# Moving four steps in the last units of an attention and soft-mixture kernel

## The chip, the core and the metric

The kernel runs on one core of one Trainium2 chip. The metric is device time in microseconds (us); lower is better. Times quoted from inside an execution are microseconds from the start of the profiled span.

## What is computed

The reference is an attention with one extra term in the softmax denominator, followed by a mixture of eight small expert networks on 32 slots:

```python
q, k, v : (8, 12, 448, 64) float32          # batch, heads, sequence, head size
scores = scale * q @ k^T ; m = max(scores, -1) ; e = exp(scores - m)
attn = e / (sum(e, -1) + exp(-m) + 1e-9) ; x = (attn @ v) as (3584, 768)
logits = x @ phi                             # phi (768, 32)
d = softmax of logits over the 3584 rows ; slot_input = d^T @ x   # 8 experts x 4 slots
slot_out[e] = relu(slot_input[e] @ w1[e]) @ w2[e]   # w1 (8,768,1024), w2 (8,1024,768)
out = softmax of logits over the 32 slots @ slot_out
```

## The kernel before

**Units and steps.** The attention is cut into 24 units `u`. A unit is two batches by two heads (six head pairs for each of four batch pairs). A unit takes seven steps `t`, one for each block of 64 positions, so step `n = 7*u + t` runs up to 168. The kernel's order is written out by hand: `at(n, where, f)` puts work into a plan, and one loop over `n` issues it in the order "small", scores of step `n`, "value", second scores of step `n - 10`, "value", "end", "load". Each engine then runs its own instructions strictly in that order and waits on semaphores.

**The stages of a unit.**
- `load_qk`, `load_v`: the loads of a unit (`load`, L124). Queries and keys are issued by POOL, values by SP, in two transfers each. All values but those of unit 23 go through the one buffer `vr`, so a load of values waits until the cast of the unit before has read it.
- `stage_T` (L226, L229): transposes of queries and keys on PE, copied out by DVE.
- `stage_S` (L238, L242, L246): scores on PE, their row maximum on DVE.
- `stage_MT` (L250 to L269): the maxima transposed on PE, copied, and spread by POOL into `md` (L258, L264).
- `stage_ST` (L276, L281, L285): the scores once more, transposed, minus the maximum, on PE; the exponential on ACT.
- `stage_V` (L290): POOL casts the unit's values to bf16 beside a column of ones. It waits for both transfers of `load_v`.
- `stage_AV` (L312): exponentials times values on PE, into one accumulator `av`.
- `stage_AVout` (L323, L326): `av` copied to `xu`, of which there is one buffer, by ACT, or by DVE for unit 22.
- `stage_den` (L332, POOL), `stage_N` (L338 reciprocal on DVE, L340 product): the normalised output `x`. L340 is "unit N's product" below. It is the last reader of `xu`, so the copy-out of the next unit waits for it. `stage_last` does the same for unit 23 on DVE.
- `stage_X` (L392, L393): `x` transposed on PE and copied, for the logits (L424).

After every six units `mixture` brings the slot softmax up to date. After the last one follow the slot inputs, the experts' hidden layer (L658), the second layer (`outer`, L762) and the combination (L819, L823), whose tiles SP writes out.

**The expert weights.** They come in 32 pieces of 768 KB (bf16; they are cast on the way by the transfer itself), all issued by POOL in `load_w` (L166). Numbers 0 to 23 are resident: they have a place of their own in `wres`, and one or two are issued per unit from unit 2 on, the last one in unit 22. Numbers 24 to 31 are called late pieces 0 to 7 here: `room(i)` gives them 3072 columns of `block`, the tile that holds the attention's working buffers, so each waits until those buffers have been read for the last time. Late piece 0 lies over `vr` and unit 21's queries and keys, piece 1 over `qr` and `kr` (there unit 23's values land, too), piece 2 over unit 22's queries and keys and `md`, piece 3 over unit 22's cast values and `xu`. Pieces 4 to 7 are needed in the last part of `outer`.

Of the kernel before, what the change touches and what calls it, by code (L numbers as in the profile page):

```python
# [23 lines left out]
def kernel(  # L24
# [10 lines left out]
    nc = tc.nc  # L35
# [7 lines left out]
    TB = S // P  # L43
# [4 lines left out]
    U = BP * HP  # L48
# [40 lines left out]
    def buf(name, i):  # L89
        o, n, bufs = parts[name]  # L90
        return block[:, ds(o + (i % bufs) * n, n)]

    def xbuf(u):
        return block[:, ds(xbuf_at((u + 4) % (HP + 1)), N2)]
# [16 lines left out]
    def room(i):  # L111

        return wres[:, i, :] if i < WRES else block[:, ds(rooms[i - WRES], HW)]
# [14 lines left out]
    def load_qk(u):  # L128

        for src, name in ((q, "qr"), (k, "kr")):  # L130
            RAW[u, name] = load(u, buf(name, 0).rearrange("p (h n) -> p h n", h=2), src, nc.gpsimd)
# [13 lines left out]
    def load_v(u):  # L145
        t_ = block[:, ds(parts["vr" if u < U - 1 else "qr"][0], 2 * N2)].bitcast(F32).rearrange("p (h n) -> p h n", h=2)
        RAW[u, "vr"] = load(u, t_, v, nc.sync if u else nc.gpsimd)
# [7 lines left out]
    def load_w(i):  # L155


        kind, e, half = weights[i]
        if kind == 1:
            J, n = KC // 2, F  # L160
            src = moe_w1[e].rearrange("(p j) f -> p j f", p=128)[:, ds(half * J, J), :]
        else:
            J, n = FK // 2, DD
            src = moe_w2[e, ds(half * 128 * J, 128 * J)].rearrange("(p j) f -> p j f", p=128)
        t_ = room(i).rearrange("p (j n) -> p j n", n=n)
        gdma(out=t_, in_=src)  # L166
        for j in range(J):
            W[kind, e, half * J + j] = t_[:, j, :]
# [51 lines left out]
    def stage_T(u, name):  # L220

        ps = slot([128, 2, S], BF16)
        r = RAW.pop((u, name))
        for t in range(TB):
            for h in range(2):
                nc.tensor.transpose(ps[ds(h * D, D), :, ds(t * P, P)],  # L226
                                    r[:, h, ds(t * D, D)], ident)
        t_ = buf(f"qk{u % 3}", 0)[:, ts(int(name == "kr"), N2)].rearrange("p (b n) -> p b n", b=2)
        nc.vector.tensor_copy(t_, ps)  # L229
        (QT if name == "qr" else KT)[u] = t_  # L230
# [17 lines left out]
    def stage_MT(u):  # L248
        ps = slot([128, 128], BF16)
        nc.tensor.transpose(ps, M[u % 2], ident)  # L250
        mt = small.tile([128, 128], BF16, tag="mt", name="mt", bufs=1)
        (nc.scalar.copy if u < U - 1 else nc.vector.tensor_copy)(mt, ps)  # L252
        em = small.tile([128, 2, TB], F32, tag="em", name="em", bufs=3)
        nc.scalar.activation(em, M[u % 2].rearrange("p (h r) -> p h r", h=2)[:, :, ds(0, TB)],
                             AF.Exp, scale=-scale)
        EM[u] = em
        md = buf(f"md{u % 2}", 0).rearrange("p (b n) -> p b n", b=2)
        nc.gpsimd.tensor_tensor(  # L258
            md[:, :, ds(0, C3 * 128)].rearrange("p b (c n) -> p b c n", c=C3),
            mt.unsqueeze(1).unsqueeze(1).broadcast_to([128, 2, C3, 128]),  # L260
            nmask[:, ds(0, 2 * C3)].rearrange("p (b c) -> p b c", b=2).unsqueeze(3)
                 .broadcast_to([128, 2, C3, 128]),
            op=ALU.mult)
        nc.gpsimd.tensor_tensor(  # L264
            md[:, :, ds(C3 * 128, P)], mt.rearrange("p (b n) -> p b n", b=2),
            nmask[:, ds(2 * C3, 1)].unsqueeze(2).broadcast_to([128, 2, P]), op=ALU.mult)
        MD[u] = md
        if u < U - 1:
            nc.gpsimd.tensor_scalar(em, em, 1e-9, None, op0=ALU.add)  # L269
# [18 lines left out]
    def stage_V(u):  # L288
        t_ = buf(f"v6{5 + u % 2}", 0).rearrange("p (h t e) -> p h t e", h=2, e=66)
        nc.gpsimd.tensor_copy(t_[:, :, :, ds(0, D)],  # L290
                              RAW.pop((u, "vr")).rearrange("p h (t d) -> p h t d", t=TB))
        if u < 2:
            nc.gpsimd.memset(t_[:, :, :, ds(D, 1)], 1.0)
        V65[u] = t_

    def stage_AV(u, ts_, part):

        for t in ts_:  # L300
            if t == 0 and part == 0:
                AV[u] = pav.tile([128, 2, 512], F32, tag="av", name="av")
            av, et = AV[u], ET[u, t]
            for h in range(2):
                for c in (range(C3) if part == 0 else (C3,)):
                    for b in range(2):
                        bs = ds(b * P, P)
                        if c < C3:
                            o, w = av[:, b, ds((h * C3 + c) * 65, 65)], 128
                        else:  # L310
                            o, w = av[bs, h, ds(2 * C3 * 65, 65)], P
                        nc.tensor.matmul(o, et[bs, h, ds(c * 128, w)],  # L312
                                         V65[u][bs, h, t, ds(0, 65)],
                                         start=(t == 0 and h == 0 and c == 0),
                                         stop=(t == TB - 1), skip_group_check=True)
            if part == 1:
                ET.pop((u, t))

    def stage_AVout(u):
        av = AV.pop(u)  # L320
        xu = buf("xu", 0).bitcast(F32).rearrange("p (h s e) -> p h s e", h=2, e=65)
        copy = nc.scalar.copy if u < U - 2 else nc.vector.tensor_copy
        copy(  # L323
            xu[:, :, ds(0, 2 * C3), :].rearrange("p h (b c) e -> p b h (c e)", b=2),
            av[:, :, ds(0, 2 * C3 * 65)].rearrange("p b (h e) -> p b h e", h=2))
        copy(xu[:, :, TB - 1, :], av[:, :, ds(2 * C3 * 65, 65)])  # L326
        XU[u] = xu

    def stage_den(u):
        xu = XU[u]  # L330
        den = small.tile([128, 2, TB], F32, tag="den", name="den")
        nc.gpsimd.tensor_tensor(den, xu[:, :, :, D], EM.pop(u), op=ALU.add)  # L332
        DEN[u] = den

    def stage_N(u):
        xv = XU.pop(u)
        rec = small.tile([128, 2, TB], F32, tag="rec", name="rec", bufs=1)
        nc.vector.reciprocal(rec, DEN.pop(u))  # L338
        x = xbuf(u).rearrange("p (s n) -> p s n", s=TB)
        (nc.gpsimd if u < U - 2 else nc.vector).tensor_tensor(  # L340
            x.rearrange("p s (h d) -> p h s d", h=2), xv[:, :, :, ds(0, D)],
            rec.unsqueeze(3).broadcast_to([128, 2, TB, D]), op=ALU.mult)
        X[u] = x
# [349 lines left out]
    def at(n, where, f):  # L693
        plan.setdefault((n, where), []).append(f)

    for u in range(U):
        n = u * TB
        if u + 1 < U:
            at(n + 5, "value", lambda u=u: [stage_T(u + 1, name) for name in ("qr", "kr")])
        if u + 2 < U:  # L700
            at(n + 5, "load", lambda u=u: load_qk(u + 2))
        at(n + 7, "value" if u < U - 1 else "small", lambda u=u: stage_MT(u))
        at(n + (9 if u < U - 1 else 5), "load", lambda u=u: stage_V(u))
        if u + 1 < U:
            at(n + (9 if u < U - 2 else 5), "load", lambda u=u: load_v(u + 1))
        for m in sorted(set(AV0)):
            at(n + m, "value", lambda u=u, m=m: [
                stage_AV(u, [t for t in range(TB) if AV0[t] == m], part) for part in range(2)])
        if u < U - 1:
            at(n + 19, "small", lambda u=u: stage_AVout(u))  # L710
            at(n + 20, "value", lambda u=u: stage_den(u))
            at(n + (23 if u < U - 3 else 22 if u < U - 2 else 21), "small", lambda u=u: stage_N(u))
        else:
            at(n + 11, "load", lambda u=u: last_sinks(u))
            at(n + 19, "small", lambda u=u: stage_last(u))
        if u < U - 2:
            at(n + 26, "value", lambda u=u: stage_X(u))
        else:
            at(n + (24 if u == U - 2 else 26), "end", lambda u=u: stage_X(u))
# [1 line left out]
        mixture(bp, (bp * HP + HP - 1) * TB + 27, at)  # L721

    for i, u in enumerate(sorted((*range(2, U - 1), 9, 13, 16))):
        at(u * TB + 5, "load", lambda i=i: load_w(i))
    at(4, "load", late_constants)
    stage_T(0, "qr")
    stage_T(0, "kr")

    end = TB * U
    for n, i in ((end - 5, 0), (end - 1, 1), (end + 3, 2), (end + 7, 3), (end + 12, 4),  # L730
                 (end + 12, 5)):
        at(n, "load", lambda i=i: load_w(WRES + i))
    at(end + 2, "load", first_spread)
# [121 lines left out]
```

## Time and profile before

| | us |
|---|---|
| median of 3 runs | 327.3 (325.09 to 332.09) |
| the profiled execution, its own time | 326.59 |
| its span, first to last instruction | 324.7 |
| PE busy in the span | 280.2 (86%) |
| DVE busy | 254.6 (78%) |
| ACT busy | 213.7 (66%) |
| POOL busy | 207.3 (64%) |

The work with units runs to about 270 us of the span, the slots and experts from there to about 295 us, and the rest writes the output. All four steps that the change touches lie between 245 and 270 us. The busy shares are means over the whole span, so they say little about that stretch; the views of the prediction are taken from it.

### The profile page before, as it was taken

The page shows a single profiled execution, that of the slowest core. Times are in us where ns is not written, and L with a number is a line of the kernel's source. Part 1 is how long each engine was busy: PE and PEld are TensorE (multiplying, and loading weights), DVE is VectorE, ACT ScalarE, POOL GpSimd, SP SyncE. Part 2 cuts the span into 40 slices and gives each one's busy share as a digit, 9 for nine tenths or more (in the row PEclk, how much of TensorE's full clock was granted, in tenths as well). Part 3 has the DMA queues.
Part 4 walks back from the last instruction along what each step waited for, and adds up shares of the span by engine and source line. Part 5 has one row for each costly group of instructions (what it writes and reads, how often), then busy time and mean ns, then how long its engine had stood idle before and what let it go on. Part 6 is the DMA issues. An engine that isn't in the chain of part 4 may idle for free.

```text
span 324.7 us, 13074 instructions
## 1 busy us (share of the span) xinstructions
PE 280.2 (86%) x5793; PEld 159.0 (49%) x5794; DVE 254.6 (78%) x354; ACT 213.7 (66%) x341; POOL 207.3 (64%) x308
## 2 busy tenths in 40 slices
PE   1669999999999988999989999998999897987910
PEld 1325555555655555556655555565555454452300
DVE  2988999898998988889989898888998844416820
ACT  3026877877778776877777778776877884216610
POOL 6356677797877786888867877968684663310000
PEclk9999999999999999999999999999999997999555
DMA  7355789998889799998997899987988599976998
GB/s 137 67 82 92 125 169 184 164 191 159 168 169 172 126 188 206 198 176 168 192 230 123 160 206 231 186 164 148 183 132 170 113 198 209 212 152 246 399 399 315
DMA packets 30311, 59.31 MB, mean 183 GB/s; under 512 B 4048, under 2 KB 22736, under 8 KB 30256
## 3 DMA queue, kind: packets, MB, share of 16 engines
q0 software_dynamic: 19056, 36.46, 65.3%
q1 hardware_dynamic: 11200, 22.02, 21.2%
q8 instruction: 45, 0.74, 0.9%
q14 instruction: 10, 0.08, 0.1%
HBM read 83.46 MB, written 11.01 MB: 291 GB/s over the span
## 4 chain that ended last, share of the span: by engine, by line
PE 57%; DVE 15%; POOL 7%; issue 6%; DMA 5%; ACT 5%; SPq 0%; ACTq 0%; POOLq 0%; DVEq 0%
PE av L312 14%; PE ps L276 10%; PE ps L238 10%; DVE m L246 8%; PE ps L281 8%; PE ps L226 6%; ACT block L285 5%; DMA block<-in_moe_w_dram 4%; PE ps L819 4%; DVE block L229 2%; PE ps L242 2%; POOL block L258 2%; POOL block L340 2%; DMA wres<-in_q_dram 1%; POOL block L124 1%
## 5 line engine op out<-in xcount | busy, mean ns | idle before, releaser
L246 DVE TENSOR_REDUCE m<-ps 128x2 bf16<-128x896 f32 x168 | 180.6, 1090 | 23.5 <-PE ps L238 19.4
L285 ACT ACTIVATE block<-ps 128x896 bf16<-128x896 f32 x168 | 153.8, 917 | 53.0 <-PE ps L281 49.1
L312 PE MATMUL av<-block 64*128 64x65 bf16 (+1 forms) x2688 | 83.7, 193 | 2.2 <-issue 1.9
L312 PEld LDWEIGHTS <-block 64*128 64x128 bf16 (+1 forms) x2688 | 70.8, 97 | 28.2 <-issue 10.1
L276 PE MATMUL ps<-block,ones 64*64 64x448 bf16 x672 | 69.1, 368 | 5.1 <-POOL block L264 2.3
L281 PE MATMUL ps<-block 64*64 64x448 bf16 x672 | 66.1, 353 | 0.2 <-issue 0.2
L238 PE MATMUL ps<-block 64*128 64x448 bf16 x288 | 54.4, 371 | 3.0 <-DVE m L246 1.3
L124 POOL DMA_DIRECT2D block<-in_q_dram x46 | 29.5, 644 | 30.9 <-PE ps L226 30.8
L238 PEld LDWEIGHTS <-block 64*128 64x128 bf16 x288 | 19.8, 94 | 52.3 <-issue 51.3
L258 POOL TENSOR_TENSOR block<-mt,nmask 128x768 bf16<-128x768 bf16 x24 | 35.7, 1487 | 9.2 <-ACT mt L252 7.8
L340 POOL TENSOR_TENSOR block<-block,rec 128x896 bf16<-128x896 f32 x22 | 37.1, 1688 | 1.4
L276 PEld LDWEIGHTS <-ones 64*64 64x64 bf16 x672 | 24.6, 105 | 10.2 <-issue 5.3
L229 DVE COPY block<-ps 128x896 bf16<-128x896 bf16 x48 | 27.8, 616 | 0.8 <-PE ps L226 0.5
L124 POOL DMA_DIRECT2D block<-in_k_dram x46 | 27.9, 627 | 0.0
L226 PE MATMUL ps<-ident,block 128*64 128x128 bf16 x644 | 25.5, 228 | 2.7 <-ACT block L285 0.5
L226 PEld LDWEIGHTS <-block 128*64 128x64 bf16 x644 | 23.0, 114 | 5.8 <-issue 2.7
L290 POOL CAST block<-block 128x896 bf16<-128x896 f32 x24 | 22.3, 931 | 3.5 <-PE ps L392 2.0
L281 PEld LDWEIGHTS <-block 64*64 64x64 bf16 x672 | 24.0, 107 | 0.6 <-issue 0.6
L323 ACT COPY block<-av 128x780 f32<-128x780 f32 x22 | 17.7, 804 | 0.0
L252 ACT COPY mt<-ps 128x128 bf16<-128x128 bf16 x23 | 6.1, 265 | 17.4 <-PE ps L250 16.8
L392 PE MATMUL ps<-ident,block 128*128 128x128 bf16 x168 | 13.4, 219 | 3.5 <-POOL block L340 1.1
L166 POOL DMA_DIRECT2D wres<-in_moe_w_dram x24 | 14.6, 617 | 1.8 <-issue 1.8
(144 smaller groups left out, 249.0 us busy)
## 6 DMA issues: line engine op xcount, KB each, us to landing
wres<-in_moe_w_dram POOLq DMA_DIRECT2D x24, 768.0 KB, 9.2
out_dram<-wres SPq DMA_DIRECT2D x28, 384.0 KB, 4.2
block<-in_v_dram SPq DMA_DIRECT2D x46, 224.0 KB, 4.6
block<-in_moe_w_dram POOLq DMA_DIRECT2D x8, 768.0 KB, 9.4
block<-in_q_dram POOLq DMA_DIRECT2D x46, 112.0 KB, 4.1
block<-in_k_dram POOLq DMA_DIRECT2D x46, 112.0 KB, 4.8
wres<-in_q_dram SPq DMA_DIRECT2D x2, 224.0 KB, 4.1
block<-in_v_dram POOLq DMA_DIRECT2D x2, 224.0 KB, 3.6
```

The costliest lines, as they stand in the source:

```text
L124: eng.dma_start(out=t_[ds(b * P, P), :, :], in_=src[bp * 2 + b, ds(hp * 2, 2)].rearrange("h (p t) d -> p h (t d)", t=TB))
L226: nc.tensor.transpose(ps[ds(h * D, D), :, ds(t * P, P)], r[:, h, ds(t * D, D)], ident)
L229: nc.vector.tensor_copy(t_, ps)
L238: nc.tensor.matmul(ps[:, h, ds(0, S)], QT[u][hs, b, ds(c * 128, 128)], KT[u][hs, b, :], start=True, stop=True)
L246: nc.vector.tensor_reduce(m[:, :, s], ps[:, :, ds(0, S)], axis=AX.X, op=ALU.max)
L258: nc.gpsimd.tensor_tensor(md[:, :, ds(0, C3 * 128)].rearrange("p b (c n) -> p b c n", c=C3), mt.unsqueeze(1).unsqueeze(1).broadcast_to([12 ...
L276: nc.tensor.matmul(ps[ds(b * P, P), h, ds(0, S)], ones[hs, :], MD[u][hs, b, :], start=True, stop=False)
L281: nc.tensor.matmul(ps[ds(b * P, P), h, ds(0, S)], KT[u][hs, b, ds(t * P, P)], QT[u][hs, b, :], start=False, stop=True)
L285: nc.scalar.activation(et, ps[:, :, ds(0, S)], AF.Exp, scale=scale)
L290: nc.gpsimd.tensor_copy(t_[:, :, :, ds(0, D)], RAW.pop((u, "vr")).rearrange("p h (t d) -> p h t d", t=TB))
L312: nc.tensor.matmul(o, et[bs, h, ds(c * 128, w)], V65[u][bs, h, t, ds(0, 65)], start=(t == 0 and h == 0 and c == 0), stop=(t == TB - 1), sk ...
L340: (nc.gpsimd if u < U - 2 else nc.vector).tensor_tensor(x.rearrange("p s (h d) -> p h s d", h=2), xv[:, :, :, ds(0, D)], rec.unsqueeze(3). ...
```

## The change

Four steps move, all in units 21 to 23:
- the last resident piece is issued at step 160 in place of 159;
- the cast of unit 22's values (the last but one) is planned at step 162 in place of 163;
- the late pieces 1 and 2 are planned at steps 166 and 170 in place of 167 and 171;
- unit 21's product (L340) goes from POOL to DVE; units 22 and 23 already had theirs there.

```diff
@@ stage_N
-        (nc.gpsimd if u < U - 2 else nc.vector).tensor_tensor(
+        (nc.gpsimd if u < U - 3 else nc.vector).tensor_tensor(
             x.rearrange("p s (h d) -> p h s d", h=2), xv[:, :, :, ds(0, D)],
             rec.unsqueeze(3).broadcast_to([128, 2, TB, D]), op=ALU.mult)
@@ the plan
-        at(n + (9 if u < U - 1 else 5), "load", lambda u=u: stage_V(u))
+        at(n + (9 if u < U - 2 else 8 if u < U - 1 else 5), "load", lambda u=u: stage_V(u))
@@
     for i, u in enumerate(sorted((*range(2, U - 1), 9, 13, 16))):
-        at(u * TB + 5, "load", lambda i=i: load_w(i))
+        at(u * TB + (5 if u < U - 2 else 6), "load", lambda i=i: load_w(i))
@@
-    for n, i in ((end - 5, 0), (end - 1, 1), (end + 3, 2), (end + 7, 3), (end + 12, 4),
+    for n, i in ((end - 5, 0), (end - 2, 1), (end + 2, 2), (end + 7, 3), (end + 12, 4),
                  (end + 12, 5)):
```

PE, ACT and SP run the same instructions in the same order. DVE has one instruction more (unit 21's product). POOL's order in the stretch, as its queue has it (den, md and product are L332, L258 with L264, and L340):

```
before: product 19, cast 21, RESIDENT, den 20, md 22, product 20, CAST 22, late 0, cast 23,
        den 21, LATE 1, md 23, PRODUCT 21, memset and copies, LATE 2, copies, den 22, late 3
after:  product 19, cast 21, den 20, RESIDENT, md 22, CAST 22, product 20, late 0, cast 23,
        LATE 1, den 21, md 23, LATE 2, memset and copies, copies, den 22, late 3
```

## The prediction

> **What bounds the kernel now.** I read the chain that ended last, backwards from the end, then each engine's timeline from 245 to 270 us, then the DMA view in windows of 1 us. The chain's last wait for a transfer, with start, duration and what:
>
> ```profile
> 277.94 0.52 POOL block L166
> 278.46 12.94 DMA block<-in_moe_w_dram
> 291.40 0.04 issue
> 291.44 1.47 PE ps L762 x29
> ```
>
> PE waits for late piece 7, which lands at 291.40. The page gives that wait as 0.84 us, so PE was ready at 290.59, and no gain from the pieces alone can pass 0.85 us. Every us by which PE itself comes later than 290.59 counts from 291.44 on; the output behind it is the same work. So two clocks matter: when PE gets there, and when piece 7 lands. The eight pieces stand back to back on the DMA engines (share 1.0 from 260 to 289). Issues and landings (median time to landing by window): piece 0 257.44 and 264.2, piece 1 259.29 and 268.3, piece 2 264.08 and 272.8, piece 3 268.52 and 276.5, then one every 3.7 us. A piece with nothing ahead lands 6.8 us after its issue (piece 0), otherwise about 4 us after the one ahead.
>
> POOL's timeline (start, duration, instruction, idle before it) shows what makes piece 0 late:
>
> ```profile
> 245.30 0.62 POOL L166 DMA_DIRECT2D wres<-in_moe_w_dram  x1
> 246.14 0.22 POOL L332 TENSOR_TENSOR den<-block,em 128x14 f32<-128x14 f32 x1 [0.22 <-ACT block L326]
> 252.56 1.69 POOL L340 TENSOR_TENSOR block<-block,rec 128x896 bf16<-128x896 f32 x1
> 256.21 0.93 POOL L290 CAST block<-block 128x896 bf16<-128x896 f32 x1 [1.97 <-PE ps L392]
> 257.44 0.61 POOL L166 DMA_DIRECT2D block<-in_moe_w_dram  x1 [0.30 <-PE ps L242]
> ```
>
> The cast at 256.21 is unit 22's. Its 1.97 us of idling is put down to PE, but PE's work for that buffer was long done; SP issued unit 22's values at 245.38 and 246.03 and they took 10.3 and 10.0 us to land (3.2 and 4.0 for unit 21's), so they landed at about 255.7 and 256.0. The cast waited for them. Unit 20's product, at 252.56, stands before that wait and ended at 254.25.
>
> PE reads that product at 255.59 (unit 20's `stage_X`), and ACT's copy-out of unit 21 (L323, 256.29) needs it, too:
>
> ```profile
> 255.59 0.56 PE L392 MATMUL ps<-ident,block 128*128 128x128 bf16 x7
> 256.45 0.38 PE L276 MATMUL ps<-block,ones 64*64 64x448 bf16 x4 [0.29 <-ACT block L285]
> 257.45 0.50 PE L312 MATMUL av<-block 64*128 64x65 bf16 x14 [0.22 <-ACT block L326]
> ```
>
> So the product has 1.34 us in hand. The change moves the cast, with its wait, in front of it.
>
> **When do unit 22's values land afterwards?** This decides the sign. They share the engines with the resident piece, issued at 245.30. One window of the DMA view, 249 to 250, and one 4 us on (packets, MB, share; q0 is POOL's queue, q1 SP's):
>
> ```profile
> q0 software_dynamic: 30, 0.18, 96.1%
> q1 hardware_dynamic: 29, 0.05, 15.8%
> ```
>
> ```profile
> q1 hardware_dynamic: 144, 0.23, 100.1%
> q0 software_dynamic: 2, 0.01, 5.9%
> ```
>
> While both queues have work they alternate packet by packet: 30 packets of the piece on 16 engines is 0.53 us each, against 0.48 without values beside it (33 in the window 231 to 232). The piece and each of the two transfers have 8 packets per engine. Two packets per us of the piece in 253 to 254 are one engine that lags: most engines were through by 251.6, this one at about 254.7, and a transfer lands only when its last engine is done.
>
> After the change the piece is issued behind unit 20's den: 246.14 + 0.22, about 246.4, 1.1 us later. Its first packets follow 1.25 us after the issue (246.55 for 245.30; 258.65 for 257.44), so at 247.6. The first transfer of values moves from about 246.6 and is through by then. The second is issued at 246.03; unit 21's second transfer, with nothing beside it, had its first packets 2.0 us after its issue, which here makes 248.0. It loses by 0.4 us and then alternates with the piece: on the prompt engines 247.6 + 1.0 (the first packet) + 7 x 0.53 = 252.3, landing about 1 us later at 253.4; if the lagging engine starts as late as before, at 255.7, as the first transfer did. Bounds: 250.0 (246.03 + 4.0, nothing in the way) and 257.3 (today's 256.2 plus the 1.1 us). I take 255.2, near the lagging engine, which gives the landing.
>
> [...]
>
> **The change, part by part.**
> 1. Cast before product. Cast from 255.2, product 0.88 later (distance of neighbours at 244.42 and 245.30) and 1.69 long: done at 257.8. PE's transposes start at 257.8 instead of 255.59: +2.2. The 0.29 us wait at 256.45 is absorbed. ACT's copy-out starts 1.5 later, less than PE's lateness, so it adds nothing. DVE's copy of the transposes and the maximum queued behind it (L246, 257.28) go 2.2 later, and with them unit 23's `stage_MT` (258.44 to 260.7): PE stays at +2.2. With the landing at 253.0 or earlier this is 0.
> 2. Unit 23's `md`: now POOL ends L264 at 261.82 and PE waits 0.29 for it. With unit 21's product gone and den behind the DMA, L258 starts when the maxima are there: 258.99 + 2.2, and ends with L264 at about 263.2, before PE comes (261.58 + 2.2). Gain 0.29.
> 3. Unit 21's product: 1.69 us less on POOL; 1.09 on DVE (row L340 DVE at 266.85), which idles 4.46 us before L323 at 263.90. That idling is AV's, ending at 263.7 on PE, not POOL's: no gain, no cost; with the cover gone 1.09. Its den goes behind piece 1's issue, about 0.6 later, into the same idling.
> 4. The piece a step later: nothing needs it before L762; its 1.1 us lie beside 30 us. SP's queue is not moved.
> 5. Pieces 1 and 2 sooner: piece 0 goes out after the product at 257.9 and lands at 264.7, piece 1 at 268.8, piece 2 (when PE has read unit 22, about 263.3) at 272.8, piece 3 (held by unit 22's product on DVE, 268.52 + 1.9) at 277.3, the rest 3.8 apart: piece 7 at 292.1. Behind piece 2 wait the memset, the copies and den 22, needed at 266.6: nothing. Alone worth 0 to 0.85.
>
> Sum: PE reaches the last part of L762 at 290.59 + 2.2 - 0.29 = 292.5, after piece 7; before, that part began at 291.44. So **+1.1 us**: 326.59 + 1.1 = 327.7. (The profiled execution's 326.59 is its span plus 1.9 and lies 0.7 below the median shown.) In general the change is the landing minus 254.1, and -1.14 at the least. Landings of 253.5 to 256.8 give 326.0 to 329.3.
>
> **Rivals.**
> - *The values win the race* (other side). Place: the second transfer on the engines at 247.6 to 248.0. If it goes ahead, it lands by 250 to 253, the cast runs right behind `md` (252.5), the product is done at 255.2, piece 0 goes out at 255.5; pieces 1 and 2 follow, piece 3 lands at 275.0, piece 7 at 289.9. PE is ready at 290.3 and waits no more: -0.85 - 0.29 = -1.14, 325.4. It decides for every landing below 254.1. For it: unit 21's second transfer needed only 4.0 us, and here it leads the piece by 0.4 us in issue. Against: the 2.0 us to its first packet, and the lagging engine.
> - *The clock falls.* A stall of 2.2 us at 255.6 may cost TensorE its clock, as an idle stretch did here (PE busy first, PEclk third from the end):
>
> ```profile
> 269.00:272.50 3.50, 2.09 (x53) 1.72 (x51) 1.70 (x6) 1.50 (x2) 1.15 (x3) 1.00 1.03 205
> 272.50:276.00 3.50, 3.14 (x15) 1.15 (x14) 2.25 (x10) 1.42 (x5) 1.38 (x1) 0.51 1.06 219
> ```
>
>   1.4 us of idling in 3.5 were followed by 3.4 us at half speed. Behind the stall PE is busy nearly throughout (3.51 of 3.80 from 258.5 to 262.3), so 3.4 us at half speed lose up to 1.7: 327.7 + 1.7 = 329.4. Against: 255.5 to 258.9 now has 2.83 of 3.41 busy, and a stall split over two such stretches may pass. [...]
> - *The piece goes first as a whole*, or the move does nothing for the values: they land at 256.1 as now, +2.0, 328.5. For it: in 117 to 121 us values issued under way got no packets until the piece ahead was through. Against: the alternation above.
>
> **How the numbers follow.** Forecast 0.42, values first 0.30, clock 0.18, piece first 0.07, else 0.03. Runs spread over 2%, about what a measurement of this kernel can tell from no change; all cases lie inside, so within 2% gets 0.94, slower 0.04 (clock lost for longer), faster 0.02. Range: from below 325.4 to above 329.4, 325.0 to 330.0; the forecast's own is 326.0 to 329.3.
>
> **What would show it.** Right: POOL idle before the cast at 252.5, the cast at about 255.2, unit 20's product ending after 257, PE idle for some 2 us before L392, no wait for a piece in L762. Wrong: the cast starting by 253 with L392 undelayed and piece 0 out by 256; a cast after 256; PEclk at half after 258.

## The result and the profile after

The changed kernel takes 330.5 us (median of 19 runs, 326.55 to 332.8), the kernel before 327.3 us (19 runs, 323.07 to 333.57). The ratio is 1.0124, with a 95% interval of 1.0095 to 1.0153: slower by about 4.0 us, where +1.1 was forecast. The time lies 0.5 us above the range. It stays within 2% of the kernel before, to which the prediction gave 0.94. Ratios, here and below, leave out the slow runs of each kernel (over 1.5% above its fastest), so they need not be the quotient of the medians.

| profiled execution | before | after |
|---|---|---|
| its own time, us | 326.59 | 329.84 |
| span, us | 324.7 | 327.9 |
| PE busy, us | 280.2 | 282.6 |

The two profiled executions differ by 3.25 us, and the account below places 2.89 of them. What separates the 3.25 us from the 4.0 us of the runs no trace shows.

To compare moments of two profiles I subtract the difference between their starts of unit 19's L392 (244.53 in before, 244.86 in after, so 0.33 for after), and write "aligned" for the result. POOL's timeline of after (start, duration, instruction, idle before it and what ended it) shows the cast waiting where the product used to run:

```profile
246.63 0.62 POOL L166 DMA_DIRECT2D wres<-in_moe_w_dram  x1
250.53 1.47 POOL L258 TENSOR_TENSOR block<-mt,nmask 128x768 bf16<-128x768 bf16 x1 [3.28 <-ACT mt L252]
256.20 0.93 POOL L290 CAST block<-block 128x896 bf16<-128x896 f32 x1 [3.39 <-DMA block<-in_v_dram]
257.11 1.68 POOL L340 TENSOR_TENSOR block<-block,rec 128x896 bf16<-128x896 f32 x1
258.74 0.60 POOL L166 DMA_DIRECT2D block<-in_moe_w_dram  x1
```

POOL idles for 3.39 us and the cast starts at 255.87 aligned, only 0.34 before its old time. PE's timeline of after, at unit 20's transposes and at the last part of `outer`:

```profile
258.84 0.93 PE L392 MATMUL ps<-ident,block 128*128 128x128 bf16 x7 [3.31 <-POOL block L340]
```

```profile
294.66 1.46 PE L762 MATMUL ps<-block,wres 128*32 128x384 bf16 x29 [0.54 <-DMA block<-in_moe_w_dram]
```

L392 waits 3.31 us for the product and starts 2.92 later than before, aligned. Its seven matmuls take 0.93 us in place of 0.56. The windows say why (length; busy time of PE, PEld, DVE, ACT and POOL; then PEclk, DMA share, GB/s):

```profile
257.30:260.80 3.50, 1.96 (x19) 1.03 (x19) 0.62 (x1) 1.17 (x3) 3.20 (x4) 0.51 0.29 25
260.80:264.20 3.40, 3.40 (x61) 1.62 (x57) 2.40 (x4) 2.41 (x4) 1.64 (x3) 0.50 0.97 195
```

For some 6.8 us TensorE was granted half its clock. The chain that ended last names the same steps:

```profile
246.35 9.70 DMA block<-in_v_dram
...
257.11 1.69 POOL block L340
...
281.86 12.77 DMA block<-in_moe_w_dram
294.66 1.48 PE ps L762 x29
```

**Where the time went,** aligned, up to the last part of L762 (291.44 before, 294.33 after, +2.89):
- the stall ahead of L392: +2.92;
- from L392 to the first matmul of unit 23's AV: 9.67 us before, 10.52 after, +0.85. It holds two opposite things. With the clock whole the changed order needs 9.1 here (9.10 and 9.11 in two experiments below), so 0.6 of small waits are gone, and the half clock costs 1.4;
- from there to L658: 14.69 before, 14.13 after, -0.56. Before, the half clock lay in this stretch (the row at 272.50 in the prediction); after, the same work runs some 3.2 us later and with the clock whole:

```profile
275.70:279.20 3.50, 2.98 (x19) 1.20 (x19) 2.64 (x11) 1.25 (x4) 1.38 (x1) 1.00 1.07 215
```

  This half clock comes and goes between executions, so the -0.56 is not shown to be the change's. Of two kernels below, the one with only the late pieces moved took 14.13 here, too (PEclk 1.00 in every window from 250.4 to 294.6), and the changed kernel with the product on POOL took 15.28, with a lower clock (PEclk 0.75 in 274.2 to 277.6 and in 277.6 to 281.0);

- the wait for piece 7: 0.84 before, 0.54 after, -0.30.

These add up to +2.91.

### The profile page after: what moved, and what is told of

It is laid out like the page before. It is cut to its first block, busy times and chain, and to the rows that moved or that the text cites. A ratio compares the mean times of both kernels' runs of the same rounds, so it can differ in the third digit from the quotient of the medians.

```text
span 327.9 us, 13076 instructions
## 1 busy us (share of the span) xinstructions
PE 282.6 (86%) x5794; PEld 159.8 (49%) x5794; DVE 256.8 (78%) x355; ACT 213.9 (65%) x341; POOL 206.4 (63%) x307
## 4 chain that ended last, share of the span: by engine, by line
PE 56%; DVE 14%; DMA 8%; POOL 7%; ACT 5%; issue 5%; SPq 0%; ACTq 0%; POOLq 0%; DVEq 0%
PE av L312 14%; PE ps L276 10%; PE ps L238 9%; DVE m L246 8%; PE ps L281 8%; PE ps L226 5%; ACT block L285 5%; PE ps L819 4%; DMA block<-in_moe_w_dram 4%; DMA block<-in_v_dram 3%; POOL block L340 2%; PE ps L242 2%; DVE block L229 2%; DMA wres<-in_q_dram 1%; POOL block L124 1%
## 5 line engine op out<-in xcount | busy, mean ns | idle before, releaser
L276 PE MATMUL ps<-block,ones 64*64 64x448 bf16 x672 | 69.9, 372 | 4.0 <-POOL block L264 2.0
L281 PE MATMUL ps<-block 64*64 64x448 bf16 x672 | 67.0, 359 | 0.0
L258 POOL TENSOR_TENSOR block<-mt,nmask 128x768 bf16<-128x768 bf16 x24 | 35.6, 1484 | 10.3 <-ACT mt L252 7.3
L340 POOL TENSOR_TENSOR block<-block,rec 128x896 bf16<-128x896 f32 x21 | 35.4, 1687 | 1.4
L276 PEld LDWEIGHTS <-ones 64*64 64x64 bf16 x672 | 24.7, 106 | 9.1 <-issue 4.1
L392 PE MATMUL ps<-ident,block 128*128 128x128 bf16 x168 | 13.9, 223 | 6.6 <-POOL block L340 4.4
L393 DVE COPY block<-ps 128x896 bf16<-128x896 bf16 (+1 forms) x23 | 14.0, 607 | 3.6 <-PE ps L392 3.5
```

What stands on the lines that cost most here:

```text
L258: nc.gpsimd.tensor_tensor(md[:, :, ds(0, C3 * 128)].rearrange("p b (c n) -> p b c n", c=C3), mt.unsqueeze(1).unsqueeze(1).broadcast_to([12 ...
L276: nc.tensor.matmul(ps[ds(b * P, P), h, ds(0, S)], ones[hs, :], MD[u][hs, b, :], start=True, stop=False)
L281: nc.tensor.matmul(ps[ds(b * P, P), h, ds(0, S)], KT[u][hs, b, ds(t * P, P)], QT[u][hs, b, :], start=False, stop=True)
L340: (nc.gpsimd if u < U - 3 else nc.vector).tensor_tensor(x.rearrange("p s (h d) -> p h s d", h=2), xv[:, :, :, ds(0, D)], rec.unsqueeze(3). ...
```

## The experiments

Names used: "cast" is unit 22's cast a step sooner, "piece" the resident piece a step later, "late" the pieces 1 and 2 sooner, "product" unit 21's product on VectorE.

**The cast alone, and everything but the cast.** The first is the kernel before with one edit, the second the changed kernel with that edit taken back.

```diff
-        at(n + (9 if u < U - 1 else 5), "load", lambda u=u: stage_V(u))
+        at(n + (9 if u < U - 2 else 8 if u < U - 1 else 5), "load", lambda u=u: stage_V(u))
```

> The kernel before with the cast alone moved (step 162). Theory: the values land at about 256 as before, the product ends near 258.8, PE idles 3 us before L392, PEclk falls to half behind it, and the time is 3 to 4.5 us above before (330.3 to 331.8). Rival (the cast's place is harmless without the other moves): within 0.5 us of before.

Measured: 329.31 us against 326.27, ratio 1.0099 (1.0062 to 1.0135). POOL's and PE's timelines show the stall of the changed kernel:

```profile
253.08 0.93 POOL L290 CAST block<-block 128x896 bf16<-128x896 f32 x1 [2.72 <-DMA block<-in_v_dram]
```

```profile
255.72 0.93 PE L392 MATMUL ps<-ident,block 128*128 128x128 bf16 x7 [2.83 <-POOL block L340]
```

Behind it PEclk is 0.51 and 0.50 in 254.4 to 257.8 and 257.8 to 261.2.

> The changed kernel with the cast of unit 22's values back behind unit 20's product (step 163); the other three moves stay. Theory (the cast's wait for the values holds up the product, the stall costs TensorE its clock): no PE idle of over 0.5 us before unit 20's transposes (L392), PEclk 1.00 from 255 to 268, the time 0 to 1 us below the kernel before (326.3 to 327.3 on its median of 327.3). Rival (the piece a step later, the product on VectorE or the late pieces cost by themselves): 329 or more.

Measured: 327.45 against 326.27, ratio 1.0034 (0.9994 to 1.0073). L392 starts without any wait, but the time did not fall below that of the kernel before, as expected. In this profile (329.98 us, above the median) PE waits 1.56 us for L264 instead, which comes behind the late casts and takes 1.14 us in place of 0.40, and its matmuls run slowly for 3.4 us behind that (from 266.5 to 269.9; the L392 at 267.36 takes 0.93 us in place of 0.56). Together: the cast's place makes nearly all of the loss, the other three parts between nothing and 0.7%.

**Is the stall's second half the clock?** Here 12 matmuls of 512 columns, which compute nothing that is used, run on PE ahead of unit 20's transposes, while the product is late.

```diff
+    def warm_slot(n=12):
+        t_ = slot([128, 2, 512])
+        for _ in range(n):
+            nc.tensor.matmul(t_[:, 0, :], ident, wres[:, 0, ds(0, 512)], start=True, stop=True)
+        return t_[:, 0, :].bitcast(BF16)[:, ds(0, N2)]
@@ stage_X
-            ps = slot([128, (b - a) * 128], BF16)
+            ps = slot([128, (b - a) * 128], BF16) if u != U - 4 else warm_slot()
```

> The changed kernel with 12 matmuls of 512 columns (2.6 us at 215 ns) put ahead of unit 20's transposes, into the same PSUM tile, which the transposes then overwrite. They lie in the stall of 3.3 us. Theory (part of the loss is the clock): PEclk 1.00 from 255 to 270, L392 still at about 258.8, and the time 1.0 to 1.7 us below the changed kernel (328.8 to 329.5 where that has 330.5). Rival (the stall is all, the half clock is hidden under the DMA wait before L762): the changed kernel's time within 0.5 us.

Measured: 328.57 against 326.27, ratio 1.009 (1.0052 to 1.0127). The profiled execution took 332.94 us, the longest of the eleven, with a pause of PE of 1.82 us ahead of the stall that the profile puts to "issue". Only the stretch behind the stall is read from it, and that ran at full clock:

```profile
257.40:260.80 3.40, 2.15 (x31) 1.03 (x31) 1.46 (x2) 1.02 (x2) 1.51 (x2) 1.00 0.20 52
260.80:264.20 3.40, 3.40 (x52) 1.76 (x49) 1.33 (x3) 1.78 (x3) 3.10 (x4) 1.00 0.32 36
```

The added matmuls took 2.76 us. The 215 ns each of the expectation agree with L618 in before, where one such matmul takes 0.38 us and three take 0.81. From L392 to unit 23's AV it took 9.10 us, after 10.52: that is the 1.4 us above. The times alone don't separate it, since the two intervals overlap; part of the gain is also given back, as the added matmuls end 0.5 us behind the product (261.88 and 262.39), and in this execution half clock came later (PEclk 0.50 in 281.0 to 284.4), so that the way from there to L658 took 15.69 us in place of 14.13. So the clock's share is shown in the trace, not in the medians.

**Three parts with the cast, without the product.** The changed kernel with unit 21's product on POOL again (`u < U - 2`).

> The changed kernel with unit 21's product back on POOL, so the other three parts of the change. Theory (the cast ahead of unit 20's product is the cost, the product on VectorE costs nothing here): PE's L392 waits about 3 us as in the changed kernel, half clock for one or two windows behind it, ratio 1.010 to 1.014. Rival (the two products beside each other on VectorE and POOL, L264 at 1.13 us in place of 0.40 and unit 21's product at 2.24 in place of 1.09, are part of the loss): ratio 1.005 to 1.009, with L264 back at 0.40 us.

Measured: 329.13 against 326.29, ratio 1.0112 (1.0064 to 1.016). POOL, PE and the windows:

```profile
255.28 0.93 POOL L290 CAST block<-block 128x896 bf16<-128x896 f32 x1 [2.63 <-DMA block<-in_v_dram]
```

```profile
257.92 0.56 PE L392 MATMUL ps<-ident,block 128*128 128x128 bf16 x7 [2.26 <-POOL block L340]
```

```profile
258.90:262.30 3.40, 3.40 (x59) 1.35 (x53) 1.71 (x4) 2.34 (x5) 2.05 (x4) 0.51 0.99 163
```

This execution is nearest to the forecast's own case: aligned (0.17 off), the cast starts at 255.1 and L392 at 257.75, 2.16 later than before, where 255.2 and +2.2 were forecast. Yet the clock falls behind a wait of 2.26 us, and the last part of L762 begins 2.25 later than before (293.69 for 291.44), not 1.1. The product's move isn't what costs.

**Is it the cast's place, or its late values?** Two kernels keep the changed order of cast and product and let the values go ahead of the piece. The first issues the piece behind unit 22's `md`, the second puts a memset of 1.38 us on POOL ahead of the piece (it writes the piece's own place, and the piece waits for it).

```diff
-        at(u * TB + (5 if u < U - 2 else 6), "load", lambda i=i: load_w(i))
+        at(u * TB + (5 if u < U - 2 else 7), "load", lambda i=i: load_w(i))
```

> The changed kernel with the last resident piece one more step later (161), which puts it behind unit 22's md on POOL, issued at about 252.8 instead of 246.6. Theory (the values are late only because the piece shares the engines with them): they land by 251, the cast starts right behind md at about 253, the product ends by 255.6, no stall, no clock drop, late piece 0 out by 256.2; time 0.5 to 1.5 us below before (325.8 to 326.8). Rival (the values are late for another reason): cast at 256, time as the changed kernel. Second rival (the piece now collides with late piece 0): no stall, but piece 7 no earlier than before, time within 0.5 us of before.

Measured: 327.07 against 326.27, ratio 1.0022 (0.9982 to 1.0063).

```profile
251.77 0.95 POOL L290 CAST block<-block 128x896 bf16<-128x896 f32 x1
```

```profile
254.43 0.56 PE L392 MATMUL ps<-ident,block 128*128 128x128 bf16 x7 [0.83 <-POOL block L340]
...
290.52 1.46 PE L762 MATMUL ps<-block,wres 128*32 128x384 bf16 x29 [2.21 <-DMA block<-in_moe_w_dram]
```

The cast waits for nothing, PE keeps its clock (L392 takes 0.56 us, not 0.93), and the gain is lost to piece 7: the resident piece now stands in front of late piece 0, and PE waits 2.21 us in place of 0.84.

```diff
-        at(u * TB + (5 if u < U - 2 else 6), "load", lambda i=i: load_w(i))
+        at(u * TB + (5 if u < U - 2 else 6), "load",
+           lambda i=i, u=u: [u == U - 2 and nc.gpsimd.memset(wres[:, i, ds(0, 1536)], 0.0), load_w(i)])
```

> The changed kernel with one memset (1536 columns, 1.38 us by the row of the memset at L538) on POOL between unit 20's den and the last resident piece; it writes the piece's own place, which the piece then overwrites. The piece goes out about 1.5 us later, its first packets some 1 us after those of the second transfer of values. Theory (the second transfer lost the engines to the piece by a few tenths of a us): both transfers go through undisturbed and land by 250.5 on the clock of the profile before, the cast starts behind md at 252.5 to 253, the product ends by 255.3, PE idles under 0.3 us before L392, no clock drop there, and the time is 0.5 to 1.2 us below before (ratio 0.996 to 0.998). Rival (the values land late whichever goes first): a stall of 2 to 3 us and the changed kernel's ratio of 1.010 or more.

Measured: 327.38 against 326.65, ratio 1.0021 (0.9979 to 1.0063). Unit 22's stall is gone (L392 waits 0.19), but the values of unit 23 now stand behind the piece, and its cast is ahead of unit 23's `md`, which PE needs at L276:

```profile
257.50 0.92 POOL L290 CAST block<-block 128x896 bf16<-128x896 f32 x1 [2.59 <-DMA block<-in_v_dram]
```

```profile
262.18 0.38 PE L276 MATMUL ps<-block,ones 64*64 64x448 bf16 x4 [2.04 <-POOL block L264]
```

So both kernels with early values come out at about 1.002, the three with late ones and no added matmuls at 1.010 to 1.012, with the same order of cast and product in all five. The loss is the late values', and the gain from their being early turns into the next wait.

**Following the wait further.** The memset kernel with unit 21's product on POOL:

> The same with unit 21's product back on POOL. Theory (beside the product on VectorE POOL's L264 takes 1.13 us in place of 0.40, and PE waits for it): L264 back at 0.4 us, PE waits nothing before unit 23's first second scores, and the time is 0 to 0.4 us below that of the kernel with the product on VectorE. Rival (POOL's 1.69 us are missed): late piece 2 goes out 1.7 us later and the time is 0.3 us or more above it.

Measured: 330.80 against 326.65, but the ratio, from three of the six runs, is 1.0009 (0.9944 to 1.0074); the six spread from 324.42 to 333.93, so this kernel settles little. PE's wait for L264 is gone, and it waits 0.84 us for piece 7, as before. Then the memset kernel with unit 23's cast behind `md` 23, and late piece 1, which needs that cast, behind both:

```diff
-        at(n + (9 if u < U - 2 else 8 if u < U - 1 else 5), "load", lambda u=u: stage_V(u))
+        at(n + (9 if u < U - 2 else 8 if u < U - 1 else 7), "load", lambda u=u: stage_V(u))
@@
-    for n, i in ((end - 5, 0), (end - 2, 1), (end + 2, 2), (end + 7, 3), (end + 12, 4),
+    for n, i in ((end - 5, 0), (end, 1), (end + 2, 2), (end + 7, 3), (end + 12, 4),
```

> The changed kernel with the memset ahead of the piece, as before, and with unit 23's cast moved behind unit 23's md (step 168 in place of 166) and late piece 1 behind that cast. Theory (every load that is late stalls whatever is queued behind its cast, so the remedy is to queue nothing urgent behind it): POOL no longer waits 2.59 us for unit 23's values ahead of md, L258 starts about 1 us sooner, PE's wait for L264 falls from 2.04 us to under 1.0, no half clock at 263 us, and the time is 0.7 to 1.5 us below that of the run with the memset alone: 0.995 to 0.999 of the kernel before. Rival (PE only waits for something else, piece 7 above all): PE's wait for L264 goes, that for piece 7 grows by the same, and the ratio stays at 1.002.

Measured: 329.19 against 326.29, ratio 1.007 (1.0028 to 1.0111): outside what either side expected. Late piece 1 went out at 270.19, after piece 0 had long landed, so the DMA engines stood empty (the DMA share is the last number but one), and PE paid at the end:

```profile
264.00:267.40 3.40, 3.40 (x75) 1.61 (x73) 2.35 (x4) 2.50 (x4) 1.05 (x2) 0.64 0.00 0
267.40:270.80 3.40, 3.40 (x102) 1.74 (x96) 1.36 (x1) 3.16 (x5) 3.02 (x5) 1.00 0.02 5
```

```profile
299.72 1.89 PE L763 MATMUL ps<-block,wres 128*32 128x384 bf16 x29 [2.51 <-DMA block<-in_moe_w_dram]
```

This execution, at 335.68 us the longest of the thirteen, also has a pause of 3.49 us on PE that the profile puts to "issue", so how much of its ratio is the empty DMA engines stays open.

**The other parts alone.** The piece a step later:

> The kernel before with the last resident piece alone a step later. Theory (the piece's own delay lets the first transfer through and puts the second behind it): the first lands in under 5 us, the second within 0.7 us of before on the clock of the profile before (255.4 to 256.8), no stall since the product stands ahead of the cast, and the time within 0.7 us of before. Rival of the prediction (the values win the race): the cast by 253 or 254 and late piece 0 out by 255.5.

Measured: 328.04 against 326.65, ratio 1.0045 (1.0005 to 1.0084). Unit 22's values landed at 256.1 aligned, as before; the piece itself at 256.0 in place of 255.4. PE waited 2.32 us for piece 7, since the pieces from 3 on landed 3 us later; in this execution PE also paused for 1.57 us ahead of AV at 255.32, which the profile puts to "issue", and its matmuls ran slowly for 3.4 us behind it (from 255.7 to 259.1; the L392 at 257.13 took 0.93 us). What the pause is, no run settles. Product and late pieces, twice:

> The kernel before with unit 21's product on VectorE and the late pieces 1 and 2 a step sooner; cast and resident piece as before. Theory (both lie in idle time): time within 0.5 us of before, L264 about 1.1 us long beside the product on VectorE, late piece 2 out some 2 us sooner without piece 7 landing sooner. Rival (the three moves other than the cast make up a good part of the loss): 1 us or more above before.

Measured: 325.88 against 326.65, ratio 0.9951 (0.9901 to 1.0), from four of six runs. It looked like a version that beats both, so it was run again with more:

> The kernel before with two parts of the change alone (unit 21's product on VectorE, late pieces 1 and 2 sooner), a second time with more rounds. Theory (these parts are worth what PE waits for piece 7 and for L264, 0.84 and 0.29 us, less what L264 loses beside the product on VectorE): 0 to 0.8 us faster, ratio 0.9975 to 1.000. Rival (the 0.995 of the first time holds): 0.993 to 0.997.

Measured: 326.28 against 326.29, ratio 1.0001 (0.9959 to 1.0043). The first result did not repeat. The late pieces alone:

> The kernel before with late pieces 1 and 2 planned a step sooner and nothing else. Theory (pieces stand back to back on the DMA engines from piece 0 on, so planning 1 and 2 sooner moves their issue and hardly their landing): piece 7 lands within 0.4 us of 291.4, ratio 0.998 to 1.001. Rival (they land sooner): piece 7 by 290.6, no wait of PE for it, ratio 0.9965 to 0.998.

Measured: 326.41 against 326.29, ratio 1.0021 (0.9987 to 1.0055). In its profile piece 7 lands at 290.4 aligned, 1.0 us sooner than before, and PE still waits 0.55 for it, as it too came sooner (with PEclk 1.00 from unit 23's AV to L658); the runs show no gain. No version here beats the kernel before.

## Why the prediction was right or wrong

- **The first half of the mechanism was right:** the cast's wait in front of unit 20's product decides the sign, POOL idles ahead of the cast, the product ends after 257, and L392 waits. All of that is in after's profile, and the experiments with the cast alone and without it show it to be the cause.
- **The landing of unit 22's values: 255.2 forecast, 255.8 measured** (aligned), so the stall is 2.92 in place of 2.2. In the kernel with the product on POOL the same step came out as forecast (255.1, 2.16), but that is luck. The forecast had the piece's move bring the values 0.9 us sooner, and the profiles show no such gain. The cast, which waits for the values, starts (aligned) at 256.2, 255.2 and 255.9 with the piece at its old step (the kernel before, the cast alone, the late pieces alone), and at 255.9, 256.3 and 255.1 with it a step later (the changed kernel, the piece alone, the product on POOL). So the landing scatters by 1 us, and the third rival's second form (0.07: the move does nothing for the values) fits the runs better than the forecast. The step behind it was wrong in its detail. It let the second transfer of values alternate with the piece at once. The DMA view of after from 249 to 250 aligned, the counterpart of the 30 and 29 packets of before:

```profile
q0 software_dynamic: 31, 0.19, 102.0%
```

  No packet of q1 at all: from 248.5 to 251 aligned the piece had 68 packets and the values 5, and only then about as many of each (27 and 26 in the us from 251). That a landing waits for the last packets is seen on the piece of before: 31 packets ran from 250 to 251, 20, 5, 2 and 2 in the four us behind that, and it landed at 255.4. The race itself was lost as forecast, by little: the piece's first packets came at 247.9, while the first transfer of values, ahead of the second on their queue, was not through before 248.1.
- **The clock: a rival with 0.18, +1.7 us; it came, at +1.4 us.** This is the step that failed: the sum put the half clock behind the stall at nothing, and the rival got too small a chance. It came as one of the prediction's own signs of being wrong, PEclk at half after 258. The argument against it, that a stall split over two stretches may pass, was an estimate that no run bears out. In every profile in which L392 waited for over 2 us (2.26, 2.83 and 3.31) the clock fell to 0.50 or 0.51 behind it, but for the kernel whose added matmuls fill the wait. The row of before that the prediction showed, half speed behind 1.4 us of idling, should have made it the likely case. Its sum, +1.1 and +1.7, is +2.8, beside the +2.89 of the trace, and that closeness is in part luck, as other terms were off and cancel. The trace lies about 1.8 us above the forecast: the clock makes 0.9 of it (1.4 less the 0.56 that did not come back), the longer stall 0.7, the wait for piece 7 0.55, and small waits take back 0.3.
- **Two smaller terms** the forecast left out or had too small: the half clock of before at 272.5 to 276 does not come back in the profile of after (-0.56, which may be chance), and small waits of PE behind L392 go (-0.6 in place of the -0.29 for `md` 23).
- **The wait for piece 7: -0.85 forecast, -0.30 measured.** Piece 3 waits for unit 22's product on DVE, which comes later with PE: forecast 1.9 later, measured 3.8 (268.52 and 272.28 aligned). The pieces behind it follow, and piece 7 landed at 294.3 aligned, not 292.1. So what delays PE here also delays the transfer that it waits for at the end. (The prediction's own spacing, four times 3.8 from 277.3, gives 292.5 for piece 7; its sum stays the same with it.)
- **Unit 21's product on DVE: free, as forecast, at another price.** It took 2.24 us in place of 1.09 and stretched POOL's L264 from 0.40 to 1.13:

```profile
263.10 1.47 POOL L258 TENSOR_TENSOR block<-mt,nmask 128x768 bf16<-128x768 bf16 x1 [1.74 <-DVE mt L252]
264.64 1.13 POOL L264 TENSOR_TENSOR block<-mt,nmask 128x128 bf16<-128x128 bf16 x1
```

```profile
263.27 2.24 DVE L340 TENSOR_TENSOR block<-block,rec 128x896 bf16<-128x896 f32 x1
```

  L258 ends at 264.57; the product needs 1.09 from there, 265.66, and ended at 265.51. L264, started at 264.64, needs 0.40 from there, 265.91, and ended at 265.77. Each reads as standing still until the other was done, and the ends agree with that within 0.15 us. With the cast taken back the two took 2.00 and 1.14 us beside each other, and with the product on POOL L264 took 0.40. Why they hold each other up, no run shows. In after all of it lay beside other work: the kernel with the product on POOL is no faster beyond the intervals (1.0112 and 1.0124). Where L264 comes last, as with the cast taken back, its 0.7 us are on PE's path.
- **The piece a step later: forecast free.** Alone it measured 1.0045, with an interval that begins at 1.0005; as it came with an unexplained pause in the profile, its price is not settled.
- **The rival on the other side** (values first, -1.14): what it needed was right, its price did not come. With the values early the stall ahead of L392 and the half clock behind it vanish, but the time stays at 1.002, as PE then waits for piece 7 or for unit 23's values. Both kernels got there by moving the piece further back, which makes those waits; values early with the piece where the change puts it, as the rival had it, no run shows.

## What to carry to other kernels

When a load's consumer is moved up an in-order queue, find out first which transfer is ahead of that load on the DMA engines, since everything queued behind the consumer inherits its wait (here 3.39 us, in front of unit 20's product). Price a stall of TensorE of 2 us or more with the half clock behind it (here 3.4 us of it behind 2.04 and 2.26, 6.8 us behind 2.83 and 3.31), unless a trace of the same kernel shows such a stall that passed at that place (here 2.21 and 2.32 ahead of L762). Before a landing is forecast to some tenths of a us, see how far it scatters: here by 1 us, whether the transfer ahead of it moved or not. And when a wait is removed, follow the buffers and pieces that come next: here two ways of having the values early gave their gain to two different later waits.

## What the runs showed of the hardware

- **The values' queue got almost nothing at first, then as many packets as the piece.** In both profiles it stood back for 1.9 and 3.1 us once the piece's packets began, and then the two moved about as many packets. Before: the piece's packets begin at 246.6, the first values' at 248.5, then 30 to 29 in a us. After: the piece at 247.9, the second values' from 251, then 27 to 26. The piece's queue was not held up in that way: its first packets at 247.9 came while the first values were still on the engines (8 of the piece and 79 of values from 247.5 to 248.0, 7 and 6 from 248.0 to 248.5).
- **Half clock behind short stalls.** A stall of 2.04 us (the memset kernel at L276) was followed by 3.4 us at half clock (PEclk 0.50 in 263.3 to 266.7), and so was that of 2.26 us (0.51 in 258.9 to 262.3); behind those of 2.83 and 3.31 us it lasted 6.8 us (0.51 and 0.50 in two windows each). But ahead of the last part of L762 the length does not tell. Behind waits of 2.21 us (the kernel with the piece behind `md` 22) and 2.32 us (the piece alone) those 29 matmuls ran at full clock (1.46 us each time); behind 2.12 us (product and late pieces, the first time) they took 2.62:

```profile
293.82 1.46 PE L762 MATMUL ps<-block,wres 128*32 128x384 bf16 x29 [2.32 <-DMA block<-in_moe_w_dram]
```

```profile
297.94 2.62 PE L762 MATMUL ps<-block,wres 128*32 128x384 bf16 x29 [2.12 <-DMA block<-in_moe_w_dram]
```

  What tells them apart, no run settles.
